# Squares and low parts of the head outputs on VectorE instead of GpSimd, inside the attention loop

## The chip, the cores and the metric

One core of a Trainium2 chip runs the whole program. The metric is device time in microseconds (us) of one execution. The core has five engines with a queue of instructions each: TensorE (PE in the profile; PEld is its weight load), VectorE (DVE), ScalarE (ACT), GpSimd (POOL) and SyncE (SP), which here issues the DMAs. An instruction at the head of a queue that has to wait holds up all that stand behind it in that queue.

## The reference

Input `x` is 1 x 2048 x 1024, 32 heads of 32 columns. Two layers are computed, each an attention block and a Fourier block, each on the layer norm of `x` and added to it:

```python
def _A_ref(x, wqkv, wo):
    qkv = (x @ wqkv).reshape(B, S, 3, H, Dh).transpose(2, 0, 3, 1, 4)
    q, k, v = qkv[0], qkv[1], qkv[2]
    scores = jnp.einsum("bhqd,bhkd->bhqk", q, k) * (Dh ** -0.5)
    p = _softmax(scores, axis=-1)
    o = jnp.einsum("bhqk,bhkd->bhqd", p, v)
    return o.transpose(0, 2, 1, 3).reshape(B, S, D) @ wo
...
x = x + _A_ref(_layernorm(x, axis=-1), A_wqkv, A_wo)
x = x + _B_ref(_layernorm(x, axis=-1), B_w_r, B_w_i)
x = x + _A_ref(_layernorm(x, axis=-1), A_wqkv, A_wo)
x = x + _B_ref(_layernorm(x, axis=-1), B_w_r, B_w_i)
```

`_B_ref` multiplies the two-dimensional Fourier transform of `x` with a fixed filter and transforms back. The change lies in the attention block only.

## The kernel before

**Number format.** Matrix products with f32 precision are made of three f16 products: a value is kept as a high part (the f16 cast, made by ScalarE) and a low part (value minus high part, made by VectorE). `split` (L167 and L168) does that for the projections, the weights and the normalised input.

**The attention loop.** The 32 heads are taken as 8 groups `g` of four. A group has 4 blocks `c` of 512 query rows, and a block 16 units `kt` of 128 key rows. For each unit TensorE makes the scores of four heads (`S`, L558) into two PSUM tiles of 128x1024, ScalarE exponentiates them (L562) into two `p` tiles in SBUF, TensorE multiplies with V (`PV`, L568), and VectorE adds the `p` tiles into two running sums for the softmax denominator (`add`, L579 and L581, in place in a region that the profile calls R). At the end of a block `fin` (L587 to L594) sums over the key partitions, inverts and scales the block's output, r; `out` (L597 to L605) keeps it as high part (`nc.scalar.copy`, L600) and low part (L601) in a tile `ohl` and stores that with a DMA on SyncE's queue (L603).

**Work between the units.** In every second unit TensorE makes a part of a projection for a later group (`filler`). There are 5 phases of projections for two groups: K or Q of one group (`qk_chunk`, 4 chunks of 24 matmuls, L340), or V of two groups (`v_tiles`, L384). All projections share one PSUM bank, `psX`, so the first matmul of a chunk waits until ScalarE and VectorE have read the chunk before: for K and Q that is the split at L343, which the profile shows at its lines L167 and L168. Behind the split stands the square of the high part (L344), in a tile `sq`. When a phase has its four chunks, `norms` (L351 to L361) sums the squares over each head's columns with four matmuls (L357) and VectorE takes the maximum (L359); from the maxima of K and Q a bound for the scores is worked out on GpSimd (`mkbias`, L363 to L370). While a phase runs, `prep` loads and splits the weights of the next one (DMA at L251); in layer 0 VectorE also takes the weights' largest value (L260, L261), a test that the program needs once.

**The output projection.** In group 6, once the projections near their end, `load_wo` (L414 to L426) brings in the 16 pieces of `wo` through a ring of three `wst` buffers (DMA at L420) and splits them into the region `big`; after them `load_o` (L435) fetches the stored head outputs `od`, and from group 7 on the output projection (L443, L466) stands between the units.

**Order.** On TensorE and ScalarE the instructions of the loop stand in the order in which the source emits them (`manual_schedule`). On VectorE, GpSimd and SyncE a scheduler in the compiler places them; each of these queues is in order, too. VectorE's queue in the loop is mostly L581, two for a unit, with the splits, `fin`, and the weights' work between them.

`both` is a list that is non-empty while the first projections are made, before the loop, and is emptied ahead of the loop (`both.clear()`).

Of the kernel before, what the change touches and what calls it, by code (L numbers as in the profile page):

```python
# [12 lines left out]
ALU = mybir.AluOpType  # L13
# [151 lines left out]
def split(nc, hi, lo, src, scale):  # L165

    nc.scalar.activation(hi, src, AF.Copy, scale=scale)  # L167
    nc.vector.scalar_tensor_tensor(lo, src, scale, hi, op0=ALU.mult, op1=ALU.subtract)  # L168
# [101 lines left out]
def attention(nc, tc, layer, ap, xin, yd, wts, wo, cst, dram, flags):  # L270
# [12 lines left out]
    both = [True]  # L283

    def bank():

        if both:
            both.append(True)
            if len(both) % 2:
                return psO.tile([128, 512], F32, name="o")  # L290
        return psX.tile([128, 512], F32, name="x")
    xhl = ap.big.bitcast(F16).rearrange("p (c a d n) -> p c a d n", a=2, d=8, n=512)
    xh, xl = ([xhl[:, c, a] for c in range(4)] for a in range(2))
    V, K, Q, bias, nrm, mx = {}, {}, {}, {}, {}, {}
# [31 lines left out]
    def qk_chunk(ph, c):  # L326
        kind, g = ph
        w = W[ph]
        if c == 0:
            if kind == "k":  # L330
                K[g] = ap.k[g % 3]
            else:
                Q[g] = qp.tile([128, 2, 2048], F16, name="Q") if g % 2 else ap.q
            p_, n_ = (qp, "Q") if ph == ("q", 0) else (sq, "sq")
            nrm[ph] = p_.tile([128, 4, 512], BF16, name="sq", tag=n_)
        t = (K if kind == "k" else Q)[g][:, :, c * 512:c * 512 + 512]
        ps = bank()
        for d in range(8):
            for i, (a, b) in enumerate(((w[:, 0, d], xh[c][:, d]), (w[:, 0, d], xl[c][:, d]), (w[:, 1, d], xh[c][:, d]))):
                nc.tensor.matmul(ps, a, b, start=d == 0 and i == 0, stop=d == 7 and i == 2)  # L340
                if d < 7 or i < 2:
                    yield
        split(nc, t[:, 0], t[:, 1], ps, SQ / (SX * SW))  # L343
        nc.gpsimd.tensor_tensor(nrm[ph][:, c], t[:, 0], t[:, 0], op=ALU.mult)  # L344
        if c == 3:
            left_norms.append(ph)
        yield
# [51 lines left out]
    def filler():  # L399
        run(prep(phases[0]))  # L400
        for i, ph in enumerate(phases):
            nxt = prep(phases[i + 1]) if i + 1 < len(phases) else iter(())
            for n in range(sums(ph)):
                yield from (v_tiles if ph[0] == "v" else qk_chunk)(ph, n)
                for _ in range(1 + (n > 0)):
                    next(nxt, None)
            run(nxt)
# [127 lines left out]
    for c in range(NCH):  # L535
        for i, ph in enumerate(PH0[1:]):
            if c < 2:
                ln(8 + 4 * c + 2 * i, 2)
            run(qk_chunk(ph, c))
        if c == 3:  # L540
            norms()
            norms()
        else:
            run(vk.pop(0))
# [49 lines left out]
        nc.vector.scalar_tensor_tensor(r, O[g, c], SO, r, op0=ALU.mult, op1=ALU.mult)  # L594
        O[g, c] = r

    def out(g, c, eng=nc.gpsimd):  # L597
        r = O.pop((g, c))
        t = on2.tile([128, 2, 512], F16, name="ohl")
        nc.scalar.copy(t[:, 0], r)  # L600
        eng.tensor_tensor(t[:, 1], r, t[:, 0], op=ALU.subtract)  # L601
        if g < NG - 1:
            nc.sync.dma_start(od[:, g, :, c * 512:(c + 1) * 512].rearrange("a p n -> p a n"), t)  # L603
        else:
            olast[c] = t  # L605
# [19 lines left out]
    with tc.manual_schedule(engines={mybir.EngineType.PE, mybir.EngineType.Activation}):  # L625
        for g in range(NG):
# [3 lines left out]
            for u in range(NCH * NKT):  # L630
                c, kt = divmod(u, NKT)
# [12 lines left out]
                if kt == 5 and done:  # L644
                    out(*done.pop())
# [11 lines left out]
                elif g == NG - 1:  # L657
                    t = rests[0] if rests else 16
# [18 lines left out]
    with tc.manual_schedule(engines={mybir.EngineType.PE}):  # L677
# [43 lines left out]
        first(0, range(7))  # L721
        fin(NG - 1, NCH - 1)
        out(NG - 1, NCH - 1, nc.vector)
        some(6)
        first(1, range(7))
# [511 lines left out]
```

## Time and profile before

| | us |
|---|---|
| median of three runs | 3907.49 |
| lowest and highest of them | 3906.37, 3912.81 |
| span of the profiled execution | 3906.3 |
| TensorE busy | 3737.0 |
| VectorE busy | 3181.5 |
| ScalarE busy | 2899.6 |
| GpSimd busy | 637.5 |

The profiled execution has no time of its own beside its span; the runs lie 0.1 to 6.5 us above it. The attention loop of layer 0 runs from about 140 to 1650 us, that of layer 1 from about 2090 to 3600 us. Times in rows are from the span's start. In a row of a timeline the first number is the start, the second how long the row lasts, xN the number of equal instructions merged into it, and the bracket the idle time of the engine just before it with what ended it. In a row of a group the numbers behind the bar are the busy time, the mean of one instruction in ns, and the idle time before them.

### The profile page before, as it was taken

To read this page: it belongs to the slowest core of one execution; us is meant where nothing else is said; L and a number is where in the kernel's file an instruction comes from. 1 tells how busy PE (TensorE), PEld (TensorE's weight loads), DVE (VectorE), ACT (ScalarE), POOL (GpSimd) and SP (SyncE) were. 2 spreads that over 40 slices of the span, in tenths; PEclk is the share of its full clock that TensorE was granted. 3 is DMA by queue.
4 is the path that set the end of the run, shared out by engine and by line. 5 is a ranking of instruction groups with operands and counts; after the bars stand their busy time and mean duration, and the time that the engine had idled before them with its cause. 6 is when DMAs were issued, how large, how long until landed. Compare 5 with 4: busy or idle time off the path is not lost.

```text
span 3906.3 us, 79627 instructions
## 1 busy us (share of the span) xinstructions
PE 3737.0 (96%) x32951; PEld 1642.5 (42%) x32951; DVE 3181.5 (81%) x3793; ACT 2899.6 (74%) x3567; POOL 637.5 (16%) x560
## 2 busy tenths in 40 slices
PE   6999999999999999989989999999999999999998
PEld 4322432342234233368853334333423432333788
DVE  6689899889998987966665998889899888788554
ACT  4577787888788865657855888888888887666686
POOL 1111011101110200014321221122121102000143
PEclk9999999999999999999999999999999999999999
DMA  8000000000000221134170000000000002111333
GB/s 203 15 12 23 12 12 17 18 12 17 15 23 7 71 71 64 64 139 142 62 176 12 15 23 12 12 18 22 10 18 12 23 12 90 52 68 66 146 97 105
DMA packets 165573, 194.07 MB, mean 50 GB/s; under 512 B 74960, under 2 KB 120656, under 8 KB 164176
## 3 DMA queue, kind: packets, MB, share of 16 engines
q1 hardware_dynamic: 164912, 188.82, 15.2%
q8 instruction: 260, 4.26, 0.4%
q14 instruction: 113, 0.93, 0.1%
q10 hardware_dynamic: 288, 0.07, 0.0%
HBM read 123.83 MB, written 48.23 MB: 44 GB/s over the span
## 4 chain that ended last, share of the span: by engine, by line
PE 75%; DVE 10%; issue 7%; ACT 4%; DMA 2%; POOL 2%; SPq 0%; DVEq 0%; ACTq 0%; POOLq 0%
PE o L568 21%; PE s L558 17%; PE x L340 13%; PE x L384 7%; PE x L443 6%; ACT p L562 2%; DVE R L581 2%; PE ps L862 2%; PE ps L800 1%; PE s L587 1%; DMA w<-in_w 1%; PE ps L791 1%; PE s L443 1%; PE ps L977 1%; PE o L384 1%
## 5 line engine op out<-in xcount | busy, mean ns | idle before, releaser
L562 ACT ACTIVATE p<-s,bias 128x1024 f32<-128x1024 f32 x2048 | 2169.0, 1111 | 589.9 <-PE s L558 578.4
L581 DVE TENSOR_TENSOR R<-R,p 128x1024 f32<-128x1024 f32 x1792 | 2146.8, 1251 | 148.3 <-ACT p L562 144.2
L568 PE MATMUL o<-p,R 128*32 128x512 f32 x8192 | 986.1, 599 | 0.0
L340 PE MATMUL x<-big,wqk 128*128 128x512 f16 x2880 | 685.6, 384 | 21.9 <-DVE R L168 8.1
L558 PEld LDWEIGHTS <-R 32*128 32x128 f16 x12288 | 232.5, 92 | 780.2 <-issue 664.6
L340 PEld LDWEIGHTS <-wqk 128*128 128x128 f16 x3072 | 277.9, 98 | 460.1 <-issue 167.5
L558 PE MATMUL s<-R 32*128 32x512 f16 x6144 | 432.5, 379 | 19.1 <-ACT p L562 15.6
L558 PE MATMUL s<-Q,R 32*128 32x512 f16 x6144 | 433.0, 378 | 11.9 <-ACT p L562 10.6
L568 PEld LDWEIGHTS o<-p,R 128*32 128x32 f32 x8192 | 213.9, 109 | 525.6 <-issue 525.0
L601 POOL TENSOR_TENSOR ohl<-zt,ohl 128x512 f16<-128x512 f32 x62 | 180.3, 2907 | 1473.6 <-ACT ohl L600 1473.6
L384 PEld LDWEIGHTS <-big 128*128 128x128 f16 x3072 | 295.0, 99 | 159.7 <-issue 79.1
L384 PE MATMUL x<-wv,big 128*128 128x256 f16 x2688 | 323.2, 277 | 40.6 <-DMA big<-hl 34.6
L579 DVE SCALAR_TENSOR_TENSOR R<-p 128x1024 f32<-128x1024 f32 x128 | 153.9, 1204 | 198.7 <-ACT p L562 198.4
L344 POOL TENSOR_TENSOR sq<-R 128x512 bf16<-128x512 f16 x96 | 144.5, 1505 | 693.8 <-ACT R L167 690.6
L443 PE MATMUL x<-big 128*128 128x512 f16 x1050 | 237.4, 380 | 0.0
L443 PEld LDWEIGHTS <-big 128*128 128x128 f16 x1344 | 126.3, 98 | 177.3 <-issue 33.9
L910 DVE TENSOR_TENSOR H<-G,H 128x512 f16<-128x512 f32 (+1 forms) x68 | 46.9, 690 | 104.7 <-ACT H L909 104.6
L862 PE MATMUL ps<-cbi,H 128*128 128x256 f16 (+1 forms) x792 | 99.2, 273 | 5.6 <-ACT H L909 3.3
L855 ACT COPY U<-ps 64x256 f32<-64x256 f32 (+1 forms) x272 | 97.0, 357 | 8.5 <-PE ps L862 3.3
L855 ACT COPY B<-ps 64x256 f32<-64x256 f32 (+1 forms) x272 | 97.0, 356 | 6.7 <-PE ps L862 3.2
L344 POOL TENSOR_TENSOR sq<-Q 128x512 bf16<-128x512 f16 x32 | 44.6, 1395 | 319.7 <-ACT Q L167 319.7
L862 PE MATMUL ps<-cb,big 128*128 128x256 f16 x780 | 96.4, 273 | 0.0
(429 smaller groups left out, 3017.1 us busy)
## 6 DMA issues: line engine op xcount, KB each, us to landing
wst<-in_wp SPq DMA_DIRECT2D x96, 256.0 KB, 3.0
R<-y SPq DMA_DIRECT2D x32, 512.0 KB, 5.4
w<-in_w SPq DMA_DIRECT2D x60, 256.0 KB, 2.6
od<-ohl SPq DMA_DIRECT2D x56, 256.0 KB, 2.4
big<-od SPq DMA_DIRECT2D x16, 896.0 KB, 6.6
y<-R SPq DMA_DIRECT2D x20, 512.0 KB, 2.7
R<-in_x SPq DMA_DIRECT2D x16, 512.0 KB, 5.6
wst<-in_wo SPq DMA_DIRECT2D x32, 256.0 KB, 2.9
```

Source lines behind the costliest of these rows:

```text
L340: nc.tensor.matmul(ps, a, b, start=d == 0 and i == 0, stop=d == 7 and i == 2)
L344: nc.gpsimd.tensor_tensor(nrm[ph][:, c], t[:, 0], t[:, 0], op=ALU.mult)
L384: nc.tensor.matmul(ps[:, j], l, r, start=d == 0 and i == 0, stop=d == 7 and i == 2)
L443: nc.tensor.matmul(p, a, b, start=start and d == ds[0] and i == 0, stop=stop and d == ds[-1] and i == 2)
L558: nc.tensor.matmul(s[h // 2][:, h % 2], K[g][r, a, kt * 128:kt * 128 + 128], Q[g][r, b, c * 512:c * 512 + 512], start=i == 0, stop=i == 2)
L562: nc.scalar.activation(p, s[hf], AF.Exp, bias=bias[g], scale=SCALE / (SQ * SQ))
L568: nc.tensor.matmul(O[g, c][32 * h:32 * h + 32], V[g][:, kt, 32 * h:32 * h + 32], P[g, c, kt, h // 2][:, h % 2], start=kt == 0, stop=kt == ...
L579: nc.vector.scalar_tensor_tensor(acc[hf], P[g, c, 0, hf], 1e-34, p, op0=ALU.add, op1=ALU.add)
L581: nc.vector.tensor_add(acc[hf], acc[hf], p)
L601: eng.tensor_tensor(t[:, 1], r, t[:, 0], op=ALU.subtract)
L855: nc.scalar.copy(ov[64 * r:64 * r + 64, a0:a0 + m, x], tl[64 * x:64 * x + 64, :m, r])
L862: nc.tensor.matmul(out, l, r, start=k == 0, stop=k == len(mm_) - 1)
```

## The change

Two instructions change their engine. In `qk_chunk` the square L344 is computed by VectorE instead of GpSimd when `both` is empty, that is in the loop (112 of the 128 squares; the 16 made ahead of the loops stay on GpSimd). In `out` the default engine of the low part L601 becomes VectorE (62 of 64; the last of each layer was on VectorE already). In the loop GpSimd keeps `mkbias` and other instructions on a few columns.

```diff
-        nc.gpsimd.tensor_tensor(nrm[ph][:, c], t[:, 0], t[:, 0], op=ALU.mult)
+        (nc.gpsimd if both else nc.vector).tensor_tensor(nrm[ph][:, c], t[:, 0], t[:, 0], op=ALU.mult)
...
-    def out(g, c, eng=nc.gpsimd):
+    def out(g, c, eng=nc.vector):
```

The orders of TensorE and ScalarE are the same in both programs. On VectorE the other instructions keep their order, and the moved ones are put between them. On VectorE at the end of a phase of K (names: R<-x is the split of a K chunk, R<-R,p an L581, zt<-oc the scaled output r, mqk the maximum):

```order
 L593 STREAM_TRANSPOSE zt<-rc 128x512
-L594 SCALAR_TENSOR_TENSOR zt<-oc,zt 128x512
-L581 TENSOR_TENSOR R<-R,p 128x1024 x12
-L168 SCALAR_TENSOR_TENSOR R<-x,R 128x512
+L344 TENSOR_TENSOR sq<-R 128x512
+L594 SCALAR_TENSOR_TENSOR zt<-oc,zt 128x512
+L581 TENSOR_TENSOR R<-R,p 128x1024 x8
+L601 TENSOR_TENSOR ohl<-zt,ohl 128x512
+L581 TENSOR_TENSOR R<-R,p 128x1024 x4
+L168 SCALAR_TENSOR_TENSOR R<-x,R 128x512
+L344 TENSOR_TENSOR sq<-R 128x512
 L581 TENSOR_TENSOR R<-R,p 128x1024 x2
```

A square now follows each split, and the subtract of a block stands behind the eighth L581 of the next block.

On VectorE while `wo` is split (big<-wst is a piece of `wo`), after the change; before, the same rows stood there without L601 and L344:

```order
L581 TENSOR_TENSOR R<-R,p 128x1024 x4
L601 TENSOR_TENSOR ohl<-zt,ohl 128x512
L168 SCALAR_TENSOR_TENSOR big<-wst,big 128x512 x2
L581 TENSOR_TENSOR R<-R,p 128x1024 x4
L168 SCALAR_TENSOR_TENSOR Q<-x,Q 128x512
L344 TENSOR_TENSOR sq<-Q 128x512
L168 SCALAR_TENSOR_TENSOR big<-wst,big 128x512 x2
```

The subtract stands ahead of two pieces of `wo`, the square ahead of two more.

SyncE's queue at the same place, before:

```order
L420 DMA wst<-in_wo 128x512 [waits DMAHW6_49,DMAHW3_49,DVE_49]
L603 DMA od_126<-ohl 128x2x512 [waits Pool_49]
L420 DMA wst<-in_wo 128x512 [waits DMAHW4_49,DVE_49]
L420 DMA wst<-in_wo 128x512 [waits DMAHW5_49,DVE_49]
L435 DMA big<-od_126 128x7x512 [waits PE_49] x2
```

and after:

```order
L420 DMA wst<-in_wo 128x512 [waits DMAHW6_49,DMAHW3_49,DVE_49]
L603 DMA od_126<-ohl 128x2x512 [waits DVE_49]
L420 DMA wst<-in_wo 128x512 [waits DMAHW4_49,DVE_49]
L420 DMA wst<-in_wo 128x512 [waits DMAHW5_49,DVE_49]
L435 DMA big<-od_126 128x7x512 [waits PE_49] x2
```

The queue keeps its order; the store L603, which stands ahead of two loads of `wo`, waits for VectorE's counter where it waited for GpSimd's.

## The prediction

> **What bounds the kernel now.** I read the busy shares first, then the chain of waits, then the table of who waited for whom, filtered to TensorE.
>
> ```profile
> PE 3737.0 (96%) x32951; PEld 1642.5 (42%) x32951; DVE 3181.5 (81%) x3793; ACT 2899.6 (74%) x3567; POOL 637.5 (16%) x560
> PE 75%; DVE 10%; issue 7%; ACT 4%; DMA 2%; POOL 2%; SPq 0%; DVEq 0%; ACTq 0%; POOLq 0%
> ```
>
> TensorE is busy 96% of the span, and its instructions are not touched. So the change can win only what TensorE idles in the loop, and lose only by making it idle more. Its waits in the loop that end on the two engines of the change, or behind them:
>
> ```profile
> PE s L558 <- ACT p L562: 26.2, 26, 6.8
> PE x L340 <- DVE R L168: 8.1, 8, 2.4
> ...
> PE s L357 <- POOL sq L344: 7.5, 5, 2.2
> ...
> PE x L340 <- DVE Q L168: 6.2, 3, 2.1
> ...
> PE x L384 <- DVE R L168: 6.0, 3, 2.1
> ...
> PE s L558 <- DVE mqk L359: 4.6, 7, 0.7
> ```
>
> Columns: total us, times, longest. The splits at L168 hold the only projection bank, so a late split stops the next projection; the squares at L344 hold the norm matmuls at L357. The first row hides two waits of almost 7 us each, which are the largest single term below.
>
> What moves, and what VectorE's rows offer as prices:
>
> ```profile
> L581 DVE TENSOR_TENSOR R<-R,p 128x1024 f32<-128x1024 f32 x1792 | 2146.8, 1251 | 148.3 <-ACT p L562 144.2
> ...
> L601 POOL TENSOR_TENSOR ohl<-zt,ohl 128x512 f16<-128x512 f32 x62 | 180.3, 2907 | 1473.6 <-ACT ohl L600 1473.6
> ...
> L344 POOL TENSOR_TENSOR sq<-R 128x512 bf16<-128x512 f16 x96 | 144.5, 1505 | 693.8 <-ACT R L167 690.6
> ```
> ```profile
> L594 DVE SCALAR_TENSOR_TENSOR zt<-oc,zt 128x512 f32<-128x512 f32 x64 | 44.2, 690 | 1.9
> ...
> L901 DVE TENSOR_TENSOR G<-ps,w 128x256 f32<-128x256 f32 x60 | 25.4, 424 | 8.0 <-PE ps L894 3.8
> ```
>
> **Prices.** The subtract L601 reads f32 over 512 columns, like L594: 0.69 us. The square L344 reads and writes 16-bit values; no such VectorE row exists. By columns it is at most 0.69 (L594), by bytes it equals 256 columns of f32, 0.42 (L901). I take 0.42, since the f32 rows grow with the words read, and keep 0.69 for the range. The Trainium skill (VectorE: DVE Perf Modes, "The perf-mode tier table (the rule you actually need)") gives tensor_tensor double rate when everything is 16-bit in SBUF: an estimate of half the column time, so the lower price and the sum as it stands below; no run here shows it yet.
>
> One L581 takes 1.22 alone. The next fence has eight of them in 9.17, so each after the first adds (9.17 - 1.22)/7 = 1.14, ends overlapping by 0.08. An inserted instruction thus costs its duration less 0.08: +0.34 for a square, +0.61 for a subtract.
>
> ```profile
> 2323.78 9.17 DVE L581 TENSOR_TENSOR R<-R,p 128x1024 f32<-128x1024 f32 x8
> 2332.86 0.69 DVE L168 SCALAR_TENSOR_TENSOR R<-x,R 128x512 f16<-128x512 f32 x1
> ...
> 2325.90 8.07 POOL L601 TENSOR_TENSOR ohl<-zt,ohl 128x512 f16<-128x512 f32 x1 [9.16 <-ACT ohl L600]
> 2333.93 2.02 POOL L344 TENSOR_TENSOR sq<-R 128x512 bf16<-128x512 f16 x1
> ...
> 2336.00 0.58 PE L357 MATMUL s<-sq,bones 128*32 128x512 bf16 x1 [2.16 <-POOL sq L344]
> ```
>
> Here GpSimd needed 8.07 for a subtract while VectorE ran freely, its square came after that, and TensorE's fourth norm matmul waited 2.16 for it. **Norm gate, three times in layer 1** (7.5 us in the table, three of 2.2): after the change a square and a subtract stand ahead of the split (+0.95), which ends at 2334.50; the square follows at 2334.84. TensorE was ready at 2333.84, so about 1.1 of the 2.16 stays. Gain 3 x 1.1 = **-3.3**.
>
> **The stores that hold the weight loads.** This is the largest term, once in each layer:
>
> ```profile
> 1342.14 9.31 POOL L601 TENSOR_TENSOR ohl<-zt,ohl 128x512 f16<-128x512 f32 x1 [9.80 <-ACT ohl L600]
> ...
> 1351.48 0.38 SPq L603 DMA_DIRECT2D od<-ohl  x1
> 1351.95 0.92 SPq L420 DMA_DIRECT2D wst<-in_wo  x2
> ...
> 1347.49 0.65 ACT L167 ACTIVATE big<-wst 128x512 f16<-128x512 f32 x1
> 1354.78 0.63 ACT L167 ACTIVATE big<-wst 128x512 f16<-128x512 f32 x1 [6.63 <-DMA wst<-in_wo]
> ...
> 1356.46 1.46 PE L558 MATMUL s<-R 32*128 32x512 f16 x10 [6.70 <-ACT p L562]
> ...
> 1340.07 4.63 DVE L581 TENSOR_TENSOR R<-R,p 128x1024 f32<-128x1024 f32 x4
> 1344.61 1.30 DVE L168 SCALAR_TENSOR_TENSOR big<-wst,big 128x512 f16<-128x512 f32 x2
> ...
> 3287.68 0.38 SPq L603 DMA_DIRECT2D od<-ohl  x1
> ...
> 3292.74 1.46 PE L558 MATMUL s<-R 32*128 32x512 f16 x10 [6.79 <-ACT p L562]
> ```
>
> GpSimd's subtract takes 9.31; the store L603 stands in SyncE's queue until 1351.48; the wo loads L420 stand behind it; ScalarE, in its fixed order, waits 6.63 for one of them; the exponentials behind wait with it, and TensorE 6.70. After the change the subtract stands behind the four L581 (order above): 1344.61 to 1345.30. The store goes at about 1345.4, the load at 1345.9. Its buffer is no later: the split that frees it starts 0.61 later than now, at 1345.2, and ends at 1345.9. So the load and its landing come 6.0 earlier; ScalarE is free at 1347.49 + 0.65 = 1348.1 and waits 0.6 more; TensorE keeps 0.7 of its 6.70. In layer 1 the store leaves at 3287.68 in the same order and the wait is 6.79: gain 2 x 6.0 = **-12.0**. If the load were held by something else the gain is nothing, and 13.5 (6.70 + 6.79) if the wait goes whole.
>
> **The late splits.** A stretch is the VectorE queue from one split to the next:
>
> ```profile
> 237.75 7.74 DVE L581 TENSOR_TENSOR R<-R,p 128x1024 f32<-128x1024 f32 x6
> ...
> 246.15 1.34 PE L340 MATMUL x<-big,wqk 128*128 128x512 f16 x4 [2.08 <-DVE Q L168]
> ...
> 287.68 5.48 DVE L581 TENSOR_TENSOR R<-R,p 128x1024 f32<-128x1024 f32 x4 [0.44 <-ACT p L562]
> 298.70 7.74 DVE L581 TENSOR_TENSOR R<-R,p 128x1024 f32<-128x1024 f32 x6
> ...
> 386.68 0.40 PE L357 MATMUL s<-sq,bones 128*32 128x512 bf16 x4
> 389.14 2.07 PE L384 MATMUL x<-wv,big 128*128 128x256 f16 x13 [2.06 <-DVE R L168]
> ...
> 2137.86 15.52 DVE L581 TENSOR_TENSOR R<-R,p 128x1024 f32<-128x1024 f32 x12
> 2153.30 0.68 DVE L168 SCALAR_TENSOR_TENSOR R<-x,R 128x512 f16<-128x512 f32 x1
> ...
> 2153.27 0.40 PE L357 MATMUL s<-sq,bones 128*32 128x512 bf16 x4
> 2154.03 1.89 PE L340 MATMUL x<-big,wqk 128*128 128x512 f16 x8 [0.36 <-DVE R L168]
> ```
>
> Undisturbed, six L581 take 1.22 + 5 x 1.14 = 6.92, four 4.64, twelve 13.76. What the rows show above that I put down to GpSimd working beside them, and it goes with its large tiles.
>
> Q split (3 waits of 2.08): one square and one subtract come in, the six get 0.82 faster: +0.34 + 0.61 - 0.82 = +0.13, times 3 = **+0.4**.
>
> Second K split (the 2.38 wait at 307 us and two like it of 1.9, in the 8.1 us): the subtract stands ahead of the earlier split, and 0.44 of idle time takes up part of it and of the square, leaving +0.51; the four give back 0.84, the six 0.82: -1.15, times 3 = **-3.4**.
>
> The K split before a V phase (3 waits, 6.0 us): +0.13 as in the first, and now the fourth norm matmul waits for the square too, which ends 0.34 after the split; with its own time and the semaphore I put 0.6 on the place: +0.7 x 3 = +2.1. The wait for the maximum (L359) behind it, 0.6 to 0.7 in the table, shrinks, since VectorE moves only 0.34 there while TensorE moves 0.6: -0.3 at two places. Together **+1.5**.
>
> The five short waits (0.36 each in the 8.1 us): twelve L581 give back 1.76 against +0.95, so the split ends 0.8 earlier, at 2153.2, the square at 2153.5, about when the fourth norm matmul is due (2153.27 + 0.3). The 0.36 goes: 5 x -0.4 = **-2.0**.
>
> Everywhere else VectorE idles before the next wait comes due, and takes up the insertions: 144 us of it in front of L581 alone (row above). If that cover were gone, each of the 112 squares and 62 subtracts would cost its 0.34 or 0.61, 38 + 38 = 76 us. The layer-1 Q splits, which wait nowhere now, get up to 0.95 later; I count nothing, and 3 x 0.95 for the range.
>
> **Sum:** -3.3 - 12.0 + 0.4 - 3.4 + 1.5 - 2.0 = **-18.8** on the profiled span of 3906.3, so 3887.5. The three runs lie 0.1 to 6.5 above that span, their median 1.2: 3888.7.
>
> **Rivals.** *The square at 0.69* (+0.27 per square ahead of a wait). Q and second K splits +0.8 each; V-phase splits, where two squares count, +1.6; norm gate +1.6; the five short ones now stall at the gate instead, 0.8 each, +4.0. Together +8.8: 3897.5 for the median. For it: no all-16-bit VectorE row. Against: bytes, as argued.
>
> *The store was not what held the loads*: the wo loads are followed by transfers of 896 KB each and by a ring of three buffers, either of which could set the landing. Then only the loop terms remain, -6.8: 3900.7. Against: load and store leave SyncE 0.47 us apart, after 6 us in which nothing left.
>
> *VectorE's queue backs up* (slower). If the long rows (7.74, 15.52) are late exponentials and not GpSimd, nothing is given back and each of the stretches pays +0.95 in full: 3 Q, 3 K and 3 layer-1 Q places 0.95 each (8.6), V-phase splits 1.5 x 3, the short waits 1.5 x 5 with the gate, less 3.3: +17. With the stores' -12 that is +5: 3912.7. It decides from a relief below about 0.3 us a stretch. For it: eight L581 beside an 8.07 us subtract were not slowed at all. Against: the bracket behind a row names a wait (0.44 for ScalarE before the four), and the six and the twelve have none.
>
> **Chances.** Forecast 0.66, square at 0.69 0.14, stores 0.12, backlog 0.08. The likeliest case's own range is 3882.5 (both big waits and the norm gate gone whole, the V-phase term at nothing: -1.5 - 3.2 - 1.5 more) to 3897. For 8 in 10 I go to **3881** (the runs' scatter below their median, 1.1, on top) **to 3903**, which takes in the two rivals that are still faster. A measurement of this kernel tells about 0.2%, 7.8 us, from no change: below 3899.7 lies nearly all of the forecast and most of the first rival, 0.76; within 0.2% 0.15; slower 0.09.
>
> **What would show it.** Right: no wo-load wait of over 1 us at ScalarE near the end of the q projections, and no 6.7 us gap at L558; L344 on VectorE near 0.42; L581's mean down from 1251 to about 1220 ns; norm matmuls waiting about 1.1 us at three places of layer 1. Wrong: six L581 still in 7.7 us, ACT still waiting over 3 us for wst<-in_wo, squares at 0.69, or new TensorE waits on L344 at places that now have none.

## The result and the profile after

| | before | after |
|---|---|---|
| median of four runs each, us | 3910.06 | 3886.24 |
| lowest and highest | 3906.37, 3912.81 | 3880.03, 3889.27 |
| span of the profiled execution | 3906.3 | 3886.0 |
| ratio after to before | | 0.9934 [0.9922, 0.9947] |

The changed kernel is 0.66% faster, by the ratio some 26 us (21 to 30). The forecast was 3888.7 in a range of 3881 to 3903; it stood on the first three of the four runs before, whose median is 3907.49.

The page of the changed kernel, busy shares and the groups of the moved work:

```profile
PE 3738.1 (96%) x32951; PEld 1644.2 (42%) x32951; DVE 3181.9 (82%) x3967; ACT 2901.1 (75%) x3567; POOL 304.1 (8%) x386
L581 DVE TENSOR_TENSOR R<-R,p 128x1024 f32<-128x1024 f32 x1792 | 2089.0, 1218 | 139.4 <-ACT p L562 136.3
```

and, from the view of groups on VectorE:

```profile
L601 DVE TENSOR_TENSOR ohl<-zt,ohl 128x512 f16<-128x512 f32 x64 | 43.7, 683 | 0.0
L344 DVE TENSOR_TENSOR sq<-R 128x512 bf16<-128x512 f16 x80 | 32.4, 405 | 0.0
```

VectorE took over 174 instructions, 62 x 0.68 + 112 x 0.41 = 88 us of work, and its busy time is unchanged (3181.5 before, 3181.9 now): L581 alone fell by 57.8 (2146.8 to 2089.0). VectorE got back from its old work what it spends on the new. Even a row on 16 columns, L591, was slowed before (mean 259 ns) and takes 168 now.

TensorE's time in the two loops, in the view of windows. Each row is one loop, from the first score matmul (L558) of a layer to its last L568; columns: window, its length, then for each engine busy time and instructions, granted clock, DMA share and rate. Before:

```profile
125.70:1655.30 1529.60, 1490.61 (x13619) 512.31 (x13618) 1354.37 (x1381) 1183.91 (x1248) 170.15 (x115) 0.99 0.08 28
...
2080.40:3592.70 1512.30, 1484.11 (x13618) 511.26 (x13618) 1326.81 (x1307) 1184.00 (x1248) 225.56 (x115) 0.99 0.08 29
```

After:

```profile
125.20:1647.30 1522.10, 1491.57 (x13618) 513.38 (x13618) 1356.21 (x1468) 1184.59 (x1248) 29.73 (x28) 0.99 0.09 28
...
2075.30:3573.50 1498.20, 1481.26 (x13618) 510.36 (x13618) 1326.61 (x1394) 1184.59 (x1248) 32.59 (x28) 1.00 0.09 29
```

Length less TensorE's busy time is what TensorE idles: 39.0 to 30.5 in layer 0, 28.2 to 16.9 in layer 1, together -19.7. The busy time of the same matmuls changed by +1.0 and -2.9, and what lies outside the loops by +1.3. That makes the 20.3 between the two spans.

Who waited for whom, of the changed kernel, TensorE's rows of layer 0 (columns as before: total us, times, longest):

```profile
PE s L558 <- ACT p L562: 8.9, 15, 1.4
PE x L340 <- DVE Q L168: 6.3, 3, 2.2
PE s L357 <- DVE sq L344: 5.9, 3, 2.0
PE x L340 <- DVE R L168: 3.2, 3, 1.7
```

and of layer 1:

```profile
PE s L558 <- ACT p L562: 7.4, 13, 1.8
...
PE s L357 <- DVE sq L344: 2.2, 3, 0.7
```

The place of the stores, layer 0 of the changed kernel (timeline; SPq is SyncE's queue, whose rows show the issue):

```profile
1341.46 0.68 DVE L601 TENSOR_TENSOR ohl<-zt,ohl 128x512 f16<-128x512 f32 x1
1342.06 1.28 DVE L168 SCALAR_TENSOR_TENSOR big<-wst,big 128x512 f16<-128x512 f32 x2
1342.17 0.38 SPq L603 DMA_DIRECT2D od<-ohl  x1
1342.77 0.93 SPq L420 DMA_DIRECT2D wst<-in_wo  x2
...
1346.71 0.63 ACT L167 ACTIVATE big<-wst 128x512 f16<-128x512 f32 x1 [1.34 <-DMA wst<-in_wo]
...
1348.40 0.82 PE L558 MATMUL s<-R 32*128 32x512 f16 x10 [1.41 <-ACT p L562]
...
1353.91 0.63 ACT L167 ACTIVATE big<-wst 128x512 f16<-128x512 f32 x1 [2.03 <-DMA wst<-in_wo]
...
1355.60 0.82 PE L558 MATMUL s<-R 32*128 32x512 f16 x10 [0.74 <-ACT p L562]
```

The subtract takes 0.68 instead of 9.31, the store leaves as it ends, and the load of `wo` leaves at 1342.77. What releases the load now is no longer the store but its buffer: the first of the two splits at 1342.06 ends 0.68 later, at 1342.74. The 6.70 at L558 is down to 1.41 here, behind ScalarE's 1.34 for the load. One piece of `wo` later TensorE has a wait that it did not have before (0.74), behind ScalarE's 2.03 for the next load; ScalarE waited 1.96 for that load before, too, but TensorE did not then wait for it.

The norm gate in layer 1 (TensorE's first three norm matmuls, the split, the fourth), timeline of the changed kernel; then the K split before a V phase, a Q split and a second K split:

```profile
2326.76 0.40 PE L357 MATMUL s<-sq,bones 128*32 128x512 bf16 x3
2326.82 0.68 DVE L168 SCALAR_TENSOR_TENSOR R<-x,R 128x512 f16<-128x512 f32 x1
...
2327.89 0.38 PE L357 MATMUL s<-sq,bones 128*32 128x512 bf16 x1 [0.73 <-DVE sq L344]
```
```profile
386.16 0.38 PE L357 MATMUL s<-sq,bones 128*32 128x512 bf16 x1 [1.95 <-DVE sq L344]
...
245.61 4.25 PE L340 MATMUL x<-big,wqk 128*128 128x512 f16 x12 [2.15 <-DVE Q L168]
...
305.78 2.75 PE L340 MATMUL x<-big,wqk 128*128 128x512 f16 x12 [1.65 <-DVE R L168]
```

The norm matmul waits 0.73 instead of 2.16; the second K split is waited for 1.65 instead of 2.38. The twelve matmuls behind the wait of 2.15 take 4.25 us, twelve of the same shape behind the wait of 1.65 take 2.75: the last section comes back to that.

### The profile page after: what moved, and what is told of

It reads as the page before. It is cut to its first block, busy times and chain, and to the rows that moved or that the text cites. A ratio compares the mean times of both kernels' runs of the same rounds, so it can differ in the third digit from the quotient of the medians.

```text
span 3886.0 us, 79635 instructions
## 1 busy us (share of the span) xinstructions
PE 3738.1 (96%) x32951; PEld 1644.2 (42%) x32951; DVE 3181.9 (82%) x3967; ACT 2901.1 (75%) x3567; POOL 304.1 (8%) x386
## 4 chain that ended last, share of the span: by engine, by line
PE 73%; DVE 12%; issue 7%; ACT 3%; DMA 3%; POOL 1%; SPq 0%; DVEq 0%; ACTq 0%; POOLq 0%
PE o L568 20%; PE s L558 17%; PE x L340 12%; PE x L384 7%; PE x L443 6%; DVE R L581 3%; ACT p L562 2%; PE ps L862 2%; PE ps L800 2%; PE s L587 1%; PE ps L791 1%; DMA w<-in_w 1%; PE s L443 1%; PE o L384 1%; PE ps L977 1%
## 5 line engine op out<-in xcount | busy, mean ns | idle before, releaser
L581 DVE TENSOR_TENSOR R<-R,p 128x1024 f32<-128x1024 f32 x1792 | 2089.0, 1218 | 139.4 <-ACT p L562 136.3
L568 PE MATMUL o<-p,R 128*32 128x512 f32 x8192 | 985.5, 599 | 0.0
L340 PE MATMUL x<-big,wqk 128*128 128x512 f16 x2880 | 684.2, 383 | 17.0 <-DVE Q L168 6.3
L558 PEld LDWEIGHTS <-R 32*128 32x128 f16 x12288 | 233.0, 92 | 769.3 <-issue 654.3
L340 PEld LDWEIGHTS <-wqk 128*128 128x128 f16 x3072 | 277.3, 98 | 452.9 <-issue 159.1
L558 PE MATMUL s<-Q,R 32*128 32x512 f16 x6144 | 433.0, 378 | 12.0 <-ACT p L562 10.7
L558 PE MATMUL s<-R 32*128 32x512 f16 x6144 | 432.3, 379 | 8.2 <-ACT p L562 6.7
L568 PEld LDWEIGHTS o<-p,R 128*32 128x32 f32 x8192 | 213.8, 109 | 524.6 <-issue 524.0
L365 POOL PARTITION_ALL_REDUCE mall<-mqk x16 | 40.7, 2542 | 2333.8 <-DVE mqk L359 2322.5
L805 DVE TENSOR_TENSOR big<-ps,big 128x512 f16<-128x512 f32 x64 | 44.5, 695 | 58.5 <-ACT big L804 58.5
L167 ACT ACTIVATE R<-x 128x512 f16<-128x512 f32 x88 | 52.7, 598 | 50.5 <-PE x L340 50.4
```

Source lines behind the costliest of these rows:

```text
L558: nc.tensor.matmul(s[h // 2][:, h % 2], K[g][r, a, kt * 128:kt * 128 + 128], Q[g][r, b, c * 512:c * 512 + 512], start=i == 0, stop=i == 2)
L568: nc.tensor.matmul(O[g, c][32 * h:32 * h + 32], V[g][:, kt, 32 * h:32 * h + 32], P[g, c, kt, h // 2][:, h % 2], start=kt == 0, stop=kt == ...
L581: nc.vector.tensor_add(acc[hf], acc[hf], p)
```

## The experiments

Each was timed beside runs of the kernel before on the same chip; ratios are to that kernel. The changed kernel was timed apart from them, so a difference to it is taken between the ratios.

**The subtract alone on VectorE** (the kernel before with the second half of the change).

```diff
-    def out(g, c, eng=nc.gpsimd):
+    def out(g, c, eng=nc.vector):
```

> Only the subtract L601 moves to VectorE; the squares stay on GpSimd. Theory (a sum of separate waits): the store of a head output no longer waits for a slow GpSimd subtract, so TensorE's waits for ScalarE at L558 fall from 26 to about 17 us, as in the full change; GpSimd is free when a square comes, so the three 2.2 us waits at the norm matmuls L357 go (-6.5); the late splits change by less than 2 us in all. Together 16 to 18 us faster than before, about 0.9955. Rival (the squares beside the L581 are what slows VectorE, and VectorE is what counts): less than half of the full change's gain, 0.997 or more, with the waits at the splits no smaller than before.

Measured: 3901.99, ratio 0.9977 [0.9967, 0.9987]; a miss, and the rival's forecast. TensorE's waits:

```profile
PE s L558 <- ACT p L562: 17.6, 28, 2.4
PE x L340 <- DVE R L168: 14.0, 16, 3.4
PE x L340 <- DVE Q L168: 8.7, 5, 2.8
```

The stores' gain is there (26.2 to 17.6), but the splits got later: 5.9 and 2.5 us more than before in the other two rows. That eats up the second gain of the theory, which came too: the norm matmuls wait 3.0 for GpSimd's squares instead of 7.5. One Q split shows why the splits are later:

```profile
239.65 5.47 DVE L581 TENSOR_TENSOR R<-R,p 128x1024 f32<-128x1024 f32 x4
...
240.47 1.30 POOL L344 TENSOR_TENSOR sq<-Q 128x512 bf16<-128x512 f16 x1 [14.75 <-ACT Q L167]
```

Four L581 take 5.47 beside one square on GpSimd, against the 4.64 of four undisturbed ones. So it was the square that slowed VectorE there, by 0.83, and the subtract's 0.61 in VectorE's queue now came on top. At the second K split, too, six L581 take 7.74, as before, beside one square of 1.87.

**The squares alone on VectorE** (the kernel before with the first half).

```diff
-        nc.gpsimd.tensor_tensor(nrm[ph][:, c], t[:, 0], t[:, 0], op=ALU.mult)
+        (nc.gpsimd if both else nc.vector).tensor_tensor(nrm[ph][:, c], t[:, 0], t[:, 0], op=ALU.mult)
```

> Only the squares L344 of the loop move to VectorE; the subtract stays on GpSimd. Theory: the waits of 6.7 us at L558 near the end of the loop's projections stay (the store still waits for a GpSimd subtract of about 9 us), the three waits of 2.2 us at L357 fall to under 0.5 us (-5 to -6), the second K splits gain about 0.5 us each; 5 to 9 us faster than before, 0.998. Rival (the squares carry the gain): 0.995 or less. Rival (VectorE is only made fuller): 0.999 to 1.002.

Measured: 3892.52, ratio 0.9953 [0.9940, 0.9967]; faster than the 0.998 expected, and nearly the rival's 0.995. The same Q split, and the stores' place:

```profile
235.03 1.17 POOL L601 TENSOR_TENSOR ohl<-zt,ohl 128x512 f16<-128x512 f32 x1 [43.33 <-ACT ohl L600]
...
236.94 6.89 DVE L581 TENSOR_TENSOR R<-R,p 128x1024 f32<-128x1024 f32 x6
...
244.49 2.75 PE L340 MATMUL x<-big,wqk 128*128 128x512 f16 x12 [1.85 <-DVE Q L168]
...
1344.31 1.46 PE L558 MATMUL s<-R 32*128 32x512 f16 x10 [7.26 <-ACT p L562]
```

GpSimd's subtract was over before the six L581 began, and they run at full speed. The stores' waits stay (7.26 here), as the theory on the stores has it. So the two halves have each their own work: the squares free the splits, the subtract frees the loads. 0.23% and 0.47% add up to about the 0.66% of the whole. A part of the second figure is clock: TensorE's clock drops, which the last section describes, are two in this trace and seven in that of the kernel before.

**The store from GpSimd's queue** (the kernel before; the store no longer stands ahead of the loads, and nothing else moves).

```diff
-            nc.sync.dma_start(od[:, g, :, c * 512:(c + 1) * 512].rearrange("a p n -> p a n"), t)
+            nc.gpsimd.dma_start(od[:, g, :, c * 512:(c + 1) * 512].rearrange("a p n -> p a n"), t)
```

> The kernel before, with the store of the head outputs (L603) issued from GpSimd's queue behind its subtract instead of from SyncE's, where it stands ahead of the loads of wo. Nothing else changes. Theory (the store held the loads): the two waits of 6.7 us at L558 fall to 2.5 us or less in each layer, 8 to 11 us faster, 0.9975; the split waits and the three norm waits stay as before. Rival (the ring of three buffers or the 896 KB transfers hold the loads): the two waits stay within 1 us of 6.7, no gain.

Measured: 3906.08, ratio 0.9990 [0.9981, 0.9999].

```profile
PE s L558 <- ACT p L562: 18.3, 30, 2.0
PE x L340 <- DVE R L168: 10.3, 8, 2.9
```

The waits of almost 7 us went (longest 2.0, total 26.2 to 18.3) although GpSimd's subtract still takes as long. That the store in SyncE's queue held the loads is shown. The time, though, fell by about 4 us, not by the 8 to 11 expected: the K splits wait 2.2 longer, and the trace has nine clock drops where the kernel before has seven. GpSimd now also issues 56 transfers, 0.79 us each; that these made the K splits late is not shown, and L581's mean hardly moved (1252 ns against 1251).

**GpSimd kept busy beside the changed kernel.** Squares and subtracts are computed by VectorE as in the change, and once more by GpSimd in four pieces of 128 columns, into a small tile that nobody reads.

```diff
...
+        if not both:
+            for j in range(4):
+                s = t[:, 0, 128 * j:128 * j + 128]
+                nc.gpsimd.tensor_tensor(ap.dum.tile([128, 128], BF16, name="dum"), s, s, op=ALU.mult)
...
+        if g < NG - 1 or c < NCH - 1:
+            for j in range(4):
+                s = slice(128 * j, 128 * j + 128)
+                nc.gpsimd.tensor_tensor(ap.dum.tile([128, 128], F16, name="dum"), r[:, s], t[:, 0, s], op=ALU.subtract)
```

> The changed kernel, with GpSimd doing the squares and subtracts a second time, in four pieces of 128 columns each, into a small tile that nothing reads. No instruction waits for it. Theory (GpSimd's tiles slow the L581 beside them): L581's mean goes from 1218 back to 1240 ns or more, the Q, K and V splits of layer 0 come later by 0.5 to 1.5 us each, the five short waits return; the store's gain stays (the L558 waits at ScalarE stay near 17 us); 5 to 15 us slower than the changed kernel, about 0.997 of before. Rival (the long L581 rows of before were late exponentials): L581's mean stays within 5 ns of 1218 and the time within 3 us of the changed kernel.

Measured: 3933.73, ratio 1.0057 [1.0043, 1.0070], some 48 us slower than the changed kernel; the direction as expected, the size far above it. In this kernel lines 340 to 601 stand 1 to 5 lines later (L586 is L581, L341 is L340):

```profile
L586 DVE TENSOR_TENSOR R<-R,p 128x1024 f32<-128x1024 f32 x1792 | 2144.1, 1250 | 118.0 <-ACT p L567 114.7
```
```profile
240.78 5.24 DVE L586 TENSOR_TENSOR R<-R,p 128x1024 f32<-128x1024 f32 x4
240.95 5.33 POOL L349 TENSOR_TENSOR dum<-Q 128x128 bf16<-128x128 f16 x4 [3.17 <-ACT Q L167]
...
246.68 4.44 PE L341 MATMUL x<-big,wqk 128*128 128x512 f16 x12 [3.30 <-DVE Q L168]
```

VectorE's queue has the same instructions as in the changed kernel, its sums are back at the mean of before (1250 against 1218 ns), and the Q split waits 3.30 instead of 2.15. The slowing is GpSimd's presence, not late exponentials: the third rival's mechanism falls. That the size is larger fits the pieces' 717.5 us on GpSimd (325.4 + 290.1 + 102.0 in their three groups), against some 370 for squares and subtracts before, beside a VectorE that now has both as well; the trace also has ten clock drops, five more than the changed kernel's. The shares were not separated.

**Four pieces of `wo` loaded ahead**, into the idle buffer of V's weights, so that the ring of three is not what the load waits for.

```diff
-            if i < 16:
+            if 10 <= i < 14:
+                st.append(early[:, i - 10])
+            elif i < 16:
...
+        early = wvp.tile([128, 4, 512], F32, name="wv")
+        for i in range(10, 14):
+            nc.sync.dma_start(early[:, i - 10], wo[i // 2 * 128:i // 2 * 128 + 128, i % 2 * 512:i % 2 * 512 + 512])
```

> The changed kernel, with pieces 10 to 13 of wo loaded ahead of all others into a buffer of their own (that of the V weights, free by then) instead of through the ring of three. Theory (after the change the ring, no longer the store, sets the last wo loads): TensorE's remaining waits for ScalarE at L558 there (1.4 and 0.7 us in layer 0, 0.3 and 1.8 in layer 1) go, and the slow clock behind the one of layer 1; 3 to 6 us faster than the changed kernel, about 0.992 of before. Rival (the bandwidth beside the 896 KB transfers sets them): the waits stay within 0.5 us, no gain.

Measured: 3886.75, ratio 0.9945 [0.9932, 0.9959]: no gain over the change; a miss. TensorE's waits behind ScalarE at L558 (there L563) fell from 17.4 to 13.5 in the whole kernel, but between 1330 and 1375 us:

```profile
PE s L563 <- DVE mqk L359: 1.8, 1, 1.8
PE x L340 <- DVE Q L168: 1.3, 1, 1.3
```

The time that TensorE no longer waits for the load it waits a few units later for VectorE, whose queue is the fuller there. The 2 to 2.6 us that the change left at each store place were not to be had by loading these four pieces earlier.

**Half of the weights' test in each layer.** In layer 0 VectorE takes the largest value of 16 weight pieces a phase (L260); the edit takes half of them there and the other half in layer 1.

```diff
-            if self.flag is not None:
+            if (self.flag is not None) if ph in PH0 else i % 2 == self.half:
...
-                nc.vector.tensor_max(self.flag, self.flag, wm)
+                nc.vector.tensor_max(self.top, self.top, wm)
...
```

> The changed kernel, with the test of the weights' largest value halved: layer 0 takes it of the even pieces and layer 1, which loads the same weights again, of the odd ones; the first phases as before. Theory (what still delays the nine late splits of layer 0 is a fixed amount of VectorE work in one stretch, and a wait of 1.8 us or more costs a slow clock on top): about 0.9 us less in each of the nine stretches, so their waits of 0.8 to 2.2 us fall to 0 to 1.3, none followed by a clock of 0.5; layer 1 gets nine new waits of 0.3 us at most; 9 to 14 us faster than the changed kernel, about 0.9905 of before. Rival (the splits wait for something else, as a DMA in front of the test): waits within 0.4 us of those of the changed kernel.

Measured: 3887.61, ratio 0.9951 [0.9938, 0.9965]: the rival was right. The Q split again (one line later than before):

```profile
236.53 0.69 DVE L261 TENSOR_REDUCE wm<-wst 128x1 f32<-128x512 f32 x1 [1.55 <-DMA wst<-in_wp]
...
245.48 4.44 PE L341 MATMUL x<-big,wqk 128*128 128x512 f16 x12 [2.49 <-DVE Q L168]
```

With one reduction instead of two, VectorE's queue stands 1.55 us for the piece that the reduction reads, and everything behind it is as late as before. It is not the reduction's 0.6 us that costs, but where it stands: ahead of the six L581 and the split, and waiting for a transfer.

**The subtract on VectorE only in group 6**, where the stores hold the loads; squares as in the change.

```diff
-    def out(g, c, eng=nc.vector):
-        r = O.pop((g, c))
+    def out(g, c, eng=None):
+        r, eng = O.pop((g, c)), eng or (nc.vector if g == NG - 2 else nc.gpsimd)
```

> Squares on VectorE as in the change, the subtract on VectorE in group 6 alone, where the loads of wo stand behind its store, and on GpSimd in the other groups. Theory (the subtract on VectorE pays only there; elsewhere it makes the split of its stretch 0.6 us later and GpSimd's own slowing of L581 is less than that): the nine waits of layer 0 as with the squares alone (1.0 to 1.9 us), the L558 waits near 18 us as in the full change, 4 to 9 us faster than the changed kernel, about 0.991 of before. Rival (the two parts add, 0.9977 and 0.9953): no faster than the changed kernel.

Measured: 3876.66, ratio 0.9917 [0.9904, 0.9931]: as expected, some 7 us faster than the change by the ratios, whose intervals overlap, and 8.3 between the spans of the two profiled executions (3877.7 and 3886.0). Of the 8.3, 6.1 is TensorE's busy time (3732.0 against 3738.1): this trace has one clock drop, that of the change five. What is left at the Q split:

```profile
237.20 0.69 DVE L260 TENSOR_REDUCE wm<-wst 128x1 f32<-128x512 f32 x1 [0.37 <-DMA wst<-in_wp]
...
246.77 3.51 PE L340 MATMUL x<-big,wqk 128*128 128x512 f16 x9 [1.92 <-DVE Q L168]
```

**The last two together** (group 6, and half of the test in each layer).

> The two preceding edits together. If both theories hold: the nine waits of layer 0 at 0.2 to 1.0 us each and no slow clock behind them, 12 to 18 us faster than the changed kernel, about 0.989 of before. If the two work on the same waits and there is nothing left for the second: as the better one of them.

Measured: 3882.87, ratio 0.9933 [0.9919, 0.9947]: a miss of both forecasts, 6 us slower than without the halving. The waits for Q grew from 6.1 in five to 8.4 in eight. The same reading as above.

**No weights' test in the loop** (group 6 as above; the maximum is left out for the weights that are loaded for the loop's phases, so part of the computation is missing and the time is a bound).

```diff
-            if self.flag is not None:
+            if self.flag is not None and ph in PH0:
```

> As with the subtract in group 6 alone, and the test of the weights' largest value left out for all phases of the loop (the first phases and wo still take it). Theory (the nine late splits of layer 0 are this test: two reductions and two maxima, 1.7 us, and 0.5 to 1.5 us in which VectorE's queue stands still until the next weights have landed): all nine waits under 0.3 us, 9 to 14 us faster than that kernel, about 0.988 of before. Rival (VectorE is late there for its whole load): waits of 0.5 us or more stay at the Q and V places.

Measured: 3850.45, ratio 0.9857 [0.9841, 0.9874], some 23 us faster than with the test by the ratios, where 9 to 14 were expected. In layer 0:

```profile
PE s L357 <- DVE sq L344: 1.5, 3, 0.5
...
PE x L340 <- DVE Q L168: 0.4, 1, 0.4
```

The late splits are gone, the loop of layer 0 takes 1497.0 us, as long as that of layer 1 (1497.2). So the nine waits of 0.8 to 2.2 us in layer 0 that the change left hang on the test. Between the two spans lie 29.3 us (3877.7 and 3848.4). Of these, 9 lie ahead of the loop (first score matmul at 117.5 instead of 126.4): with the test, three reductions of weights for the loop stand there already, and VectorE idles 10.1 in front of them for their transfers. Another 19 lie in the loop of layer 0. Of these 19, 10 are idle time (28.0 to 17.6) and 8 TensorE's busy time. Some 3 of the 8 are clock: in this loop it stands at 0.50 for 10.2 us with the test and for 3.4 without, half of which is lost. The rest stays open.

**The test on the high part** (group 6 as above). The whole computation, with one difference: the maximum is taken of the f16 high part `h` that ScalarE makes (scaled back by 1/SW), not of the loaded piece, so the reduction stands behind the split's first half and not behind the transfer.

```diff
-                nc.vector.tensor_reduce(wm, st[i], axis=AX.XY, op=ALU.max, apply_absolute_value=True)
-                nc.vector.tensor_max(self.flag, self.flag, wm)
+                nc.vector.tensor_reduce(wm, h, axis=AX.XY, op=ALU.max, apply_absolute_value=True)
+                nc.vector.scalar_tensor_tensor(self.flag, wm, 1.0 / SW, self.flag, op0=ALU.mult, op1=ALU.max)
```

> As with the subtract in group 6 alone, and the test reads the high part in f16 (256 times the weight, scaled back) instead of the loaded piece, so that it stands behind the split that it needs anyway and never waits for a transfer. All of the computation is kept. Theory (half of what delays the nine splits is the wait for the transfer, not the work): no wait in front of L260 in the loop, the nine waits 0.3 to 1.1 us instead of 0.7 to 1.9, layer 1 unchanged; 5 to 9 us faster than that kernel, about 0.990 of before. Rival (only the amount of work counts): no more than 2 us faster.

Measured: 3861.91, ratio 0.9886 [0.9869, 0.9902]: 45 us faster than the kernel before, some 19 than the change and 12 than with the subtract in group 6 alone, where 5 to 9 were expected. The group and the Q split:

```profile
L260 DVE TENSOR_REDUCE wm<-wqk 128x1 f32<-128x512 f16 x32 | 21.6, 675 | 0.0
```
```profile
230.88 8.03 DVE L581 TENSOR_TENSOR R<-R,p 128x1024 f32<-128x1024 f32 x7
...
239.56 2.75 PE L340 MATMUL x<-big,wqk 128*128 128x512 f16 x12 [0.77 <-DVE Q L168]
```

The reduction costs as much as before (675 ns against 680), but VectorE never waits ahead of it, and the split's wait falls from 1.92 to 0.77. Of the 17.0 us between the spans of this version and the one with the subtract in group 6 alone (3860.7 and 3877.7), 6.4 lie ahead of the loop (first score matmul at 120.0 instead of 126.4), where the waits of 10.1 are gone, too. It is the best of the versions that compute everything.

## Why the prediction was right, and where its steps were not

The total was right (20.3 us between the spans against 18.8; by the ratio the gain is a little larger, 21 to 30 us), by terms of which some were too large and some too small. That they meet so closely is partly luck: the 3.2 that the stores gave too much are made up by 2.2 at the V phases, 1.2 at L359 and 1.0 at the norm gate. TensorE's waits in the loops, from the view of waits, loop by loop:

| term | predicted | measured | |
|---|---|---|---|
| norm gate, layer 1 | -3.3 | -4.3 | 6.5 to 2.2 |
| stores that hold the `wo` loads | -12.0 | -8.8 | 13.5 to 4.7 |
| Q splits | +0.4 | +0.1 | 6.2 to 6.3 |
| second K splits | -3.4 | -3.0 | 6.2 to 3.2 |
| K split before a V phase, gate | +2.1 | -0.1 | 6.0 to 5.9 |
| wait for the maximum, L359 | -0.6 | -1.8 | 4.5 to 2.7 |
| five short waits | -2.0 | -1.8 | 1.8 to 0 |
| sum | -18.8 | -19.7 | |

**Prices.** The square costs 0.41 on VectorE (0.42 taken, the rival's 0.69 falls), the subtract 0.68 (0.69 taken). The Trainium skill (VectorE: DVE Perf Modes, "The perf-mode tier table (the rule you actually need)") gives a `tensor_tensor` on 16-bit values in SBUF the double rate, which is the square's case, and one on f32 the single rate; 0.41 for the square against 0.68 for the subtract, which reads and writes f16 beside its f32, agrees.

**Stores.** The mechanism was right: the wait behind the store, the queue and its order are as described, and the store alone, taken from SyncE's queue, removes the waits too. The size was too large. The step that failed is "ScalarE is free at 1348.1 and waits 0.6 more; TensorE keeps 0.7 of its 6.70". The load itself takes longer: ScalarE starts on the piece 3.94 us after the load's issue (1342.77 to 1346.71), where it was 2.83 before (1351.95 to 1354.78), and waits 1.34. And the ring behind that load was not followed: ScalarE waits 2.03 for the next piece. TensorE keeps 2.6 in layer 0 (1.41, 0.74 and an earlier 0.41) and 2.1 in layer 1. Why the load takes longer stays open.

**Norm gate.** Right in mechanism. 0.73 is left of 2.16 and not 1.1. The step that was off is the +0.95 ahead of the split: it was to end 0.66 after TensorE was ready (2334.50 against 2333.84), and ends 0.34 after (2326.82 + 0.68 against 2326.76 + 0.40), so a third of it had been taken up earlier in VectorE's queue.

**The V-phase splits.** The mechanism is the one predicted: the fourth norm matmul, and not the split, is what TensorE waits for (1.95 at 386.16). The 0.7 a place was too much. The prediction gave the L581 alone back to VectorE; rows like L591 got faster as well. Whether these paid for the rest was not separated.

**What slowed VectorE.** The prediction put the long L581 rows down to "GpSimd working beside them", without parting squares from subtracts, and the expectations of the first two experiments parted them the wrong way. At the splits that were looked at, the squares slowed the L581; at the Q split the subtract was over before them. Over the whole kernel the two slow L581 alike: its mean is 1218 ns with neither on GpSimd, 1227 with the subtracts, 1228 with the squares, 1251 with both. It is the place that tells them apart. In the splits' stretches the subtract's move seems to have cost time (the group-6 version is some 7 us faster than the change, much of it clock), and it paid where its store held the `wo` loads.

**Rivals.** The square at 0.69, the store not being the cause, and the backlog of VectorE are each contradicted by a row: 405 ns, the experiment on the store, and L581's mean of 1218.

## What to carry to other kernels

An instruction that moves to a busy engine can be free or better when the engine it leaves was slowing the busy one: look for the same instruction's duration with and without a neighbour at work, place by place, and move only where a late result is waited for. Where an in-order queue has a store of a slow producer ahead of loads, follow the loads to the last one of the ring before sizing the gain. And an instruction that reads a freshly loaded buffer in the middle of a busy in-order queue can cost more by its position than by its duration: a reduction that takes the same data from a later copy gained some 12 us here, a part of it ahead of the loop.

## What was not expected of the hardware

TensorE runs slow for some us after a short stall. The kernel before, view of windows (the clock is the third number from the end; the second is TensorE's busy time). The first two rows stand around the wait of 2.08 that ends at 246.15, the next three around another of the three waits for Q, which is as long and ends at 616.98; the last stands behind the wait of 6.70 at 1356 us:

```profile
243.31:246.72 3.41, 1.33 (x15) 1.00 0.00 0
246.72:250.13 3.41, 3.41 (x10) 0.50 0.02 5
...
611.94:615.36 3.42, 2.97 (x36) 1.00 0.00 0
615.36:618.77 3.41, 1.79 (x9) 1.00 0.00 0
618.77:622.18 3.41, 3.41 (x33) 1.00 0.00 0
...
1356.50:1359.50 3.00, 3.00 (x14) 0.84 (x14) 3.00 (x3) 2.87 (x3) 0.00 (x0) 0.51 1.08 377
```

The granted clock is 0.50 for 3.41 us behind the first wait and stays at 1.00 behind the second. The rows with and without the drop were shown above: twelve projection matmuls take 2.75 after waits of 0.77, 1.65 and 1.85, and 4.25, 4.44 and 4.44 after waits of 2.15, 2.49 and 3.30, some 1.5 us more. In these traces the drop followed every wait near 7 us and about half of those of 1.8 to 2.5, and almost none of under 1.6. Besides one at the start of each loop, the kernel before has seven such drops, the changed one five, two fewer in layer 1, which is where its busy time fell by 2.9.

The traces show what parts two waits of one length. In each trace the clock changes only at the edges of a grid of steps of 3.41 us. The first wait lies within one step, which leaves TensorE 1.33 busy of 3.41; the second is cut by an edge into 0.45 and 1.63. Past their first 30 us, the loops of all twelve traces hold 166 stalls of over 0.7 us. Where TensorE idled 2.0 us or more of one step, the clock dropped in 36 cases of 36; from 1.6 to 2.0, in 15 of 30; below 1.6, in 1 of 100. What tips the cases in between was not found, and no run moves a stall within its step on purpose. Against the program's start the grid lies at another place in most traces (from 0.02 to 3.34 us), so which stalls of about 2 us cost a drop is partly chance, and with it a part of the differences between versions above.

So a stall of 2 us can cost nearly twice its length, and the prediction, which counted idle time alone, had no term for it. The Trainium skill (TensorE: Matmul & The Clock Gate, "Part 1: The HAM clock gate (the "warmup" mystery)") describes a clock that drops after idle time and recovers under load; the rows agree with that, at gaps shorter than the window of about 3.4 us that it names. It adds that the window runs free of the program; the grid in these traces agrees with that. That the scatter between runs of one kernel comes from such drops fits the clocks on record (of the changed kernel's runs, the one of 3880.03 has a mean granted clock of 0.991, the other three 0.988 or 0.989), and was not tested.
